# Sums of exponentials read over 112 columns, one divisor operation, partition copies on GpSimd, and a new instruction order, in a fused attention and gated MLP kernel

## The chip, the cores and the metric

The kernel runs on one core of a Trainium2 chip. Its time is the device time of one launch in microseconds. Three runs gave 727.54, 728.48 and 729.30 us, median 728.48.

Engines are named as in the profile: PE is TensorE's matrix multiply, PEld its weight load, DVE is VectorE, ACT is ScalarE, POOL is GpSimd, SP is the engine that issues nearly all DMAs.

## The reference

Eight batches, twelve heads, 448 positions, head size 64. Attention with a soft cap, then a gated MLP with a spatial product, all in float32:

```python
scores = matmul(q, k.T) / sqrt(64)
scores = cap * tanh(scores / cap)
attn = exp(scores - max(scores))
attn = attn / (sum(attn) + 1e-9)
x = matmul(attn, v)                      # heads side by side: 448 x 768
h = maximum(x @ w_in, 0)                 # 448 x 1024
u, v = h[:, :512], h[:, 512:]
v_n = (v - mean(v)) / sqrt(var(v) + 1e-6)
v_s = w_spatial @ v_n + b_spatial[:, None]
out = (u * v_s) @ w_out                  # 448 x 768
```

## The kernel before, in words

**Two programs.** One branch serves a small cap, where exp needs no maximum subtracted beforehand; the other serves any cap. The branch is taken once, on the chip. All that is told here is of the first (`bounded`).

**Attention, `pair_bnd` (L556).** Heads are worked two at a time: six pairs per batch, 48 in all. Scores are computed transposed, keys on partitions and 448 queries of two heads on columns, in 64-row by 64-column tiles of the PE array (L593, 56 matmuls of 224 columns a pair, each in two passes in the trace). ACT takes tanh into `tp` (key blocks 0 to 3) and `tq` (blocks 4 to 6) (L600) and exp in place (L605). PE multiplies with the values (L615) into `ps_x`, again in 64 by 64 tiles; ACT copies that to `xf` (L620).

**The divisor.** The maximum of the exponentials is always made on DVE (L647 four tensor operations, L658 a 32 by 32 transpose, L660 a reduce into `st`). It is needed for the 1e-9 term. The sum of the exponentials is made on PE for the first ten pairs (`PE_SUMS = 10`, all of batch 0 and four pairs of batch 1), by products with a matrix of ones (L640): for each of seven key blocks, four products of 128 columns that lie side by side in four 32-column strips of the array, one for each head and each of two overlapping groups of 32-query blocks. ACT copies the result to `sx` (L644). One of the ten (pair 5, `FAST`) goes on through PE; the other nine go through DRAM: `sx` to `sd` to `dq` by DMA. For those nine, DVE then moves the upper halves of `st` to other partitions (L705, two copies of 32 by 14), takes the maximum (L714), forms the divisor in two operations (L711) and its reciprocal (L716), and two more DMA steps bring the reciprocal to all partitions as `rr`. In the other 38 pairs DVE makes the sums too.

**The MLP, `moe` (L784).** `xf` times `rr` (L773) is split in two float32r parts `xg` (ACT or DVE, L352, L348, and for batch 0 a copy of 64 columns on DVE, L354). PE computes u and v (L806 to L808, L828 to L833), the spatial product (L901 to L906) and the output (L926 to L928) with three float32r products for each, on the whole 128 by 128 array. The weights are split from float64 in the first 120 us, on POOL (L419), DVE (L423 to L426, L348) and ACT (L352).

**What sets the order.** Every step is a `Plan` task with an engine, a duration, a key and the buffers it needs. `Plan.order` (L75) plays the tasks through a list scheduler once, on the host: an idle engine takes the ready task of the smallest key, PE adds `STICK` to the key of a task whose array mode differs from the last one's, and POOL and some DVE tasks exclude each other. The result is one fixed order for each engine; on the chip each engine runs its list in order and waits on semaphores. The keys are the tables `BND_KEY`, `KEY0`, `KEY1`, `KEY7` (added for batches 0, 1 and 7) and `BND_W_KEYS`.

Of the kernel before, what the change touches and what calls it, by code (L numbers as in the profile page):

```python
# [18 lines left out]
FH = DF // 2  # L19
# [26 lines left out]
class Plan:  # L46
# [7 lines left out]
    TURN, STICK = {"N": 111.0, "K": 95.0, "R": 190.0, "C": 100.0, "Q": 100.0}, 11.80957  # L54
# [174 lines left out]
BND_KEY = dict(tr=-300.859619, ld=66.923828, vld=74.281982, sc=-6.748779, th=-13.830078, ex=-614.690186, pv=1.041748, sm=26.029053, mx=26.478027, dn=31.365723, ev=-123.362305, x=5.41333, moe=9.348389, span=8.481445, step=0.303955, mv=-3.17041)  # L229
KEY0 = dict(tr=59.859619, ld=-206.415527, vld=-222.091553, sc=-619.906494, th=-404.370117, ex=637.646729, pv=-43.61792, sm=472.690186, mx=-388.116455, dn=-437.234619, ev=-178.652832, x=-259.482666, moe=-7.794922, mv=-2.662842)  # L230
KEY1 = dict(tr=409.030762, ld=-17.121582, vld=-89.626709, sc=-8.86792, th=-12.678955, ex=103.096191, pv=-3.411865, sm=-34.066406, mx=-33.196045, dn=-141.463135, ev=-64.928467, x=-7.304688, moe=-0.158936, mv=-9.574707)
KEY7 = dict(tr=-794.004639, ld=1184.412354, vld=279.873779, sc=0.273438, th=878.253174, ex=671.313232, pv=-1.608398, sm=35.75708, mx=35.69043, dn=-2.840088, ev=359.308594, x=2.395508, moe=-0.6604, mv=169.783203)
BND_V_FIRST = 1
WARM, WARM_N = 7, 480
BND_W_KEYS = -12.596436, 0.300049, -1.349609, -18.415039, 10.094727
# [9 lines left out]
VH3 = True  # L245
# [3 lines left out]
def attn_moe(ctx, tc, bounded, shared, qk, v, qk2, v2, cap, w_in, w_sp, w_out, out):  # L249
# [12 lines left out]
    const = pool("const", 1)  # L262
    if bounded and VH3:
        TAGS = {**TAGS, "vh": (512, F32R, 3)}
# [298 lines left out]
    def pair_bnd(b, hp, xf):  # L563
# [67 lines left out]
        if by_pe:  # L631
            acc, sx = Buf("acc"), Buf("sx")
            bank = lambda: acc.t[:, 0]
            sides = [(k, e) for k in range(2) for e in range(2)]

            def ones():
                for c in range(NC):
                    for s, (k, e) in enumerate(sides):
                        o = bank()[s * 32:(s + 1) * 32, :128]
                        nc.tensor.matmul(o if fast else o.rearrange("p (i b) -> p b i", b=4), lhsT=one, rhs=part(c, e)[:, k * 96:k * 96 + 128],  # L640
                                         start=(c == 0), stop=(c == NC - 1))

            z1 = add("T", 1540, kk("pv", 1) + 0.01, ones, exps, [*tps, acc], [acc], name="ones", mode="Q")
            z1 = add("A", act(128), kk("ev"), lambda: nc.scalar.copy(out=sx.t, in_=bank()[:, :128]), [z1], [acc, sx], [sx], name="sev")  # L644
# [49 lines left out]
        if by_pe and SHIFT:  # L694
# [4 lines left out]
                       [sx, sd], [sd], lat=XL)  # L699
            sums = [add("S", HW, kk("dn"), lambda h=h: nc.sync.dma_start(  # L700
                out=dq.t[half_h(h), :16].rearrange("p (s b) -> p s b", b=4),
                in_=sd.t.rearrange("(s h i b) -> h i s b", h=2, i=32, b=4)[h]), [sums], [sd, dq], [dq] if h == 0 else [], lat=XL) for h in range(2)]

            def shift(h):
                nc.vector.tensor_copy(low(0)[half_h(h)], st.t[h * D + 32:h * D + D, :QB])  # L705

            def den(k):
                b = slice(0, 4) if k == 0 else slice(4, 7)
                i, o = (low(j).rearrange("p (e b) -> p e b", e=2)[:, :, b] for j in (1, 2))
                a = dq.t[:96, :16].rearrange("p (s b) -> p s b", b=4)[:, 2 * k:2 * k + 2, k:]  # L710
                nc.vector.scalar_tensor_tensor(o, i, EPS_ATTN, a, op0=ALU.mult, op1=ALU.add)  # L711

            d = [add("V", 90, kk("dn"), lambda h=h: shift(h), [*done, sums[0]], [st, dq], name="shift") for h in range(2)]
            d = add("V", 90, kk("dn"), lambda: nc.vector.tensor_tensor(low(1), st.t[:96, :QB], low(0), op=ALU.max), d, [st, dq], name="mred2")  # L714
            d = [add("V", 105, kk("dn"), lambda k=k: den(k), [d, *sums], [dq], name="den") for k in range(2)]
# [43 lines left out]
    def pair(b, hp):  # L759
# [16 lines left out]
        t = add(E_X[3], ct(E_X[3], D), k, lambda: copy(E_X[3], g.t[:, S:XH], xf.t[:, S - D:]), [m, c], [xf, g], name="xt")  # L776
# [10 lines left out]
    def moe(b, xs):  # L787
# [27 lines left out]
        def v_part():  # L815


            for t in range(4):
                k = next(ks)
                acc, vr, ls, vh, vl = Buf(next(tags)), Buf("stg"), Buf("lst"), Buf("vh3" if bounded and VH3 and t == 3 else "vh"), Buf("vl")  # L820
                ts, last = slice(t * 128, (t + 1) * 128), t == 3

# [192 lines left out]
```

## Time and profile before

| What | Time (us) |
|---|---|
| median of three runs | 728.48 |
| the profiled execution | 728.05 |
| its span, first to last instruction | 726.3 |
| PE busy | 712.7 |
| DVE busy | 603.0 |
| ACT busy | 475.2 |
| POOL busy | 40.0 |

The profiled execution lies 0.43 us under the median. PE is busy 98% of the span, at the full granted clock all through (1.00 in every stretch until the last matmul). Busy time counts a matmul from start to end, and matmuls overlap, so a busy PE may still lose time where it changes between tile shapes; that is read from start times.

### The profile page before, as it was taken

The numbers are of one execution on the slowest core, as the hardware profiler recorded it, in microseconds if no ns is written. First come the engines' busy times: TensorE is split into PE (matmuls) and PEld (weight loads), VectorE is DVE, ScalarE is ACT, GpSimd is POOL, SyncE is SP. The second block draws the span as 40 slices with busy tenths as digits, with TensorE's granted clock in tenths as the row PEclk, the third lists the DMA queues.
The fourth block names the chain that finished last, engine by engine and source line by source line (L and its number), as shares of the span: only waits on it lengthen the run. The fifth ranks groups of instructions, "written<-read, shape, count | busy, mean of one in ns | idle before, by whom it ended". The sixth has DMA issues, their size and how long they took to land.

```text
span 726.3 us, 19114 instructions
## 1 busy us (share of the span) xinstructions
PE 712.7 (98%) x8001; PEld 596.5 (82%) x8001; DVE 603.0 (83%) x1187; ACT 475.2 (65%) x658; POOL 40.0 (6%) x57
## 2 busy tenths in 40 slices
PE   8998999999999999999999999999999999999997
PEld 5776788788898888887788887988889887888896
DVE  4999999999998999797997899978988869874530
ACT  7998757876829848479466676576582874572321
POOL 2301110000100010000100000000000001000100
PEclk9999999999999999999999999999999999999999
DMA  7577724443404414135133443144241441212002
GB/s 262 177 209 232 220 59 122 136 144 93 128 19 155 153 34 130 53 130 157 37 97 92 128 120 76 58 129 141 69 130 28 143 123 65 66 41 98 8 0 81
DMA packets 53286, 78.87 MB, mean 109 GB/s; under 512 B 24956, under 2 KB 37830, under 8 KB 53190
## 3 DMA queue, kind: packets, MB, share of 16 engines
q1 hardware_dynamic: 53044, 77.55, 35.7%
q8 instruction: 65, 1.06, 0.6%
q14 instruction: 31, 0.25, 0.1%
q10 hardware_dynamic: 146, 0.00, 0.0%
HBM read 65.76 MB, written 11.76 MB: 107 GB/s over the span
## 4 chain that ended last, share of the span: by engine, by line
PE 81%; DVE 10%; ACT 3%; DMA 3%; issue 1%; POOL 0%; SPq 0%; ACTq 0%; DVEq 0%; POOLq 0%
PE ps_s L593 14%; PE ps_x L615 14%; PE ps_acc L926 5%; PE ps_acc L928 5%; PE ps_acc L927 5%; PE ps_acc L806 4%; PE ps_acc L808 4%; PE ps_acc L807 4%; PE ps_acc L831 4%; PE ps_acc L833 4%; PE ps_acc L832 4%; DVE red L647 4%; PE ps_acc L904 2%; PE ps_acc L906 2%; PE ps_acc L905 2%; PE ps_acc L828 1%
## 5 line engine op out<-in xcount | busy, mean ns | idle before, releaser
L647 DVE TENSOR_TENSOR red<-red,tq 128x896 f32<-128x896 f32 (+1 forms) x172 | 141.9, 847 | 24.1 <-ACT tq L605 24.1
L593 PE MATMUL ps_s<-raw 64*64 64x224 f32 x2688 | 147.8, 353 | 3.3 <-ACT tp L600 1.4
L593 PEld LDWEIGHTS ps_s<-raw 64*64 64x64 f32 x2688 | 98.1, 133 | 39.4 <-ACT tp L600 5.8
L600 ACT ACTIVATE tp<-ps_s,capt 128x896 f32<-128x896 f32 x96 | 92.0, 1012 | 3.5 <-PE ps_s L593 2.3
L647 DVE TENSOR_TENSOR red<-tp 128x896 f32<-128x896 f32 x86 | 90.6, 1077 | 4.4 <-ACT tp L605 4.4
L605 ACT ACTIVATE tp<-tp,capt 128x1792 f32<-128x1792 f32 x48 | 86.6, 1804 | 0.5
L615 PE MATMUL ps_x<-tp,v 64*64 64x224 f32 x1536 | 81.6, 350 | 1.5 <-ACT tp L605 1.2
L600 ACT ACTIVATE tq<-ps_s,capt 128x896 f32<-128x896 f32 x96 | 73.7, 822 | 10.6 <-PE ps_s L593 9.3
L615 PEld LDWEIGHTS ps_x<-tp,v 64*64 64x64 f32 x1536 | 57.8, 133 | 17.2 <-ACT tp L605 1.6
L605 ACT ACTIVATE tq<-tq,capt 128x1344 f32<-128x1344 f32 x48 | 68.4, 1425 | 0.9
L926 PE MATMUL ps_acc<-xg,wo_h 128*128 128x448 f32 x176 | 64.6, 367 | 0.0
L615 PE MATMUL ps_x<-tq,v 64*64 64x224 f32 x1152 | 63.2, 349 | 1.1 <-ACT tq L605 1.1
L806 PE MATMUL ps_acc<-xg,wiu_h 128*128 128x448 f32 x174 | 64.0, 368 | 0.0
L928 PE MATMUL ps_acc<-xg,wo_l 128*128 128x448 f32 x176 | 63.8, 363 | 0.0
L927 PE MATMUL ps_acc<-xg,wo_h 128*128 128x448 f32 x176 | 63.5, 361 | 0.0
L808 PE MATMUL ps_acc<-xg,wiu_l 128*128 128x448 f32 x174 | 63.1, 363 | 0.0
L807 PE MATMUL ps_acc<-xg,wiu_h 128*128 128x448 f32 x174 | 62.7, 360 | 0.0
L773 DVE TENSOR_TENSOR xf<-xf,rr 128x448 f32<-128x448 f32 x47 | 29.0, 618 | 30.5 <-DMA rr<-rd 21.6
L855 POOL TENSOR_TENSOR lst<-lst,capt 128x1 f32<-128x1 f32 x32 | 21.6, 678 | 585.2 <-DVE lst L853 481.7
L615 PEld LDWEIGHTS ps_x<-tq,v 64*64 64x64 f32 x1152 | 43.9, 133 | 11.9 <-ACT tq L605 1.5
L658 DVE STREAM_TRANSPOSE red<-red 128x448 f32<-128x448 f32 x85 | 52.7, 632 | 0.6
L647 DVE TENSOR_TENSOR red<-red 128x448 f32<-128x448 f32 x86 | 52.2, 620 | 0.2
(144 smaller groups left out, 1298.1 us busy)
## 6 DMA issues: line engine op xcount, KB each, us to landing
v<-in_v SPq DMA_DIRECT2D x48, 448.0 KB, 4.7
raw<-in_qk SPq DMA_DIRECT2D x47, 448.0 KB, 4.4
out<-o SPq DMA_DIRECT2D x48, 224.0 KB, 2.3
rr<-rd SPq DMA_DIRECT2D x94, 112.0 KB, 3.1
w<-in_w_in SPq DMA_DIRECT2D x12, 512.0 KB, 5.0
xg<-in_w_out SPq DMA_DIRECT2D x12, 256.0 KB, 2.9
wy<-in_w_sp SPq DMA_DIRECT2D x3, 224.0 KB, 3.3
md<-st SPq DMA_DIRECT2D x38, 14.0 KB, 1.7
```

The costliest lines, as they stand in the source:

```text
L593: nc.tensor.matmul(ps.t[half_rows(h), e, c % 2 * QH:(c % 2 + 1) * QH], lhsT=raw.t[half_rows(e), S + c * D:S + (c + 1) * D], rhs=raw.t[half ...
L600: lambda o=g % 2 * PW, w=w, ps=ps, tp=tp: nc.scalar.activation(out=tp.t[:, o:o + 2 * w].rearrange("p (e q) -> p e q", e=2), in_=ps.t[:, :, ...
L605: lambda tp=tp, w=w: nc.scalar.activation(out=tp.t[:, :w], in_=tp.t[:, :w], func=AF.Exp, scale=ca), [ex], [tp],
L615: nc.tensor.matmul(inat(x.t[half_rows(e), h, :QH]), lhsT=vt.t[half_rows(h), (2 * c + e) * D:(2 * c + e + 1) * D], rhs=part(c, e)[half_rows ...
L647: tt = lambda o_, i0, i1, op=op: nc.vector.tensor_tensor(o_, i0, i1, op=op)
L658: d = add("V", dve(S) + 26, kk(key), lambda r=r, one_=one_: nc.vector.transpose(out=blk(r.t[:, :S]), in_=blk(one_())), [d], [r], name="vtr")
L806: nc.tensor.matmul(ps, lhsT=wiu_h[:, c, fs], rhs=x[:, XH:], start=(c == 0), stop=False)
L807: nc.tensor.matmul(ps, lhsT=wiu_h[:, c, fs], rhs=x[:, :S], start=False, stop=False)
L808: nc.tensor.matmul(ps, lhsT=wiu_l[:, c, fs], rhs=x[:, XH:], start=False, stop=(c == NP - 1))
L926: nc.tensor.matmul(ps, lhsT=wo_h[:, c, ns], rhs=g[:, XH:], start=(c == 0), stop=False)
L927: nc.tensor.matmul(ps, lhsT=wo_h[:, c, ns], rhs=g[:, :S], start=False, stop=False)
L928: nc.tensor.matmul(ps, lhsT=wo_l[:, c, ns], rhs=g[:, XH:], start=False, stop=(c == 3))
```

## The change

It has four parts.

**Ones.** For the nine pairs that go through DRAM, each product with ones reads 16 of the 32 queries of each of all seven 32-query blocks (112 columns in seven runs of 16) instead of four whole blocks (128 columns in one run). `sx` has 112 columns, the two heads go to `sd` in two DMAs, and each of the two DMAs to `dq` waits for its own.

**Divisor.** With that layout the divisor is one operation over 14 columns where there were two, over 8 and 6.

**Partition copies.** The two copies of `st` to other partitions (`E_SHIFT`), and in batch 0 the copy of 64 columns of `xf` into `xg` (`E_XT`), are issued on POOL instead of DVE.

**Order.** All key tables have new values, so the order changes on every engine for batches 0, 1 and 7 above all. The other new names (`LN_A`, `ST_A`, `RL_A`) are zero and change nothing.

```diff
-    TURN, STICK = {"N": 111.0, "K": 95.0, "R": 190.0, "C": 100.0, "Q": 100.0}, 11.80957
+    TURN, STICK = {"N": 111.0, "K": 95.0, "R": 190.0, "C": 100.0, "Q": 100.0}, 12.158936
-BND_KEY = dict(tr=-300.859619, ld=66.923828, vld=74.281982, ...
+BND_KEY = dict(tr=-120.344971, ld=111.291992, vld=156.294922, ...
...
-VH3 = True
+E_SHIFT, E_DEN, E_XT, E_EPS = "P", "V", "P", "V"
+SMALL = 150
+LN_A, ST_A, RL_A, VH3, W112 = 0, 0, 0, True, True
...
-            sides = [(k, e) for k in range(2) for e in range(2)]
+            sides = [(k, e) for k in range(2) for e in range(2)] if not W112 or fast else [(k, e) for e in range(2) for k in range(2)]
...
+                        if W112 and not fast:
+                            nc.tensor.matmul(o[:, :QC].rearrange("p (i b) -> p b i", b=QB // 2), lhsT=one,
+                                             rhs=part(c, e).rearrange("p (b i) -> p b i", i=32)[:, :, k * 16:k * 16 + 16],
+                                             start=(c == 0), stop=(c == NC - 1))
+                            continue
                         nc.tensor.matmul(o if fast else o.rearrange("p (i b) -> p b i", b=4), lhsT=one, rhs=part(c, e)[:, k * 96:k * 96 + 128],
                                          start=(c == 0), stop=(c == NC - 1))
...
-            z1 = add("T", 1540, kk("pv", 1) + 0.01, ones, exps, [*tps, acc], [acc], name="ones", mode="Q")
+            z1 = add("T", 1360 if W112 and not fast else 1540, kk("pv", 1) + 0.01, ones, exps, [*tps, acc], [acc], name="ones", mode="Q")
...
             def shift(h):
-                nc.vector.tensor_copy(low(0)[half_h(h)], st.t[h * D + 32:h * D + D, :QB])
+                copy(E_SHIFT, low(0)[half_h(h)], st.t[h * D + 32:h * D + D, :QB])
 
             def den(k):
+                if W112:
+                    nc.vector.scalar_tensor_tensor(low(2), low(1), EPS_ATTN, dq.t[:96, :QB], op0=ALU.mult, op1=ALU.add)
+                    return
...
-        t = add(E_X[3], ct(E_X[3], D), k, lambda: copy(E_X[3], g.t[:, S:XH], xf.t[:, S - D:]), [m, c], [xf, g], name="xt")
+        e_xt = E_XT if bounded and E_X[3] == "V" else E_X[3]
+        t = add(e_xt, SMALL + 30 if e_xt == "P" else ct(e_xt, D), k, lambda: copy(e_xt, g.t[:, S:XH], xf.t[:, S - D:]), [m, c], [xf, g], name="xt")
```

Where the instructions now stand is shown at three places. The first is ACT's list at the end of the first stage, where attention of batch 0 runs out and the first MLP product follows on PE (`tp` and `tq` are exponentials, `ps_s` the scores, `wiv_h` and `wiu_h` weight parts, `xg` a finished pair). Before:

```order
L605 ACTIVATE tq<-tq,capt 128x1344
L620 COPY xf<-ps_x 128x448
L352 CAST wiv_h<-wy 128x512
L600 ACTIVATE tp<-ps_s,capt 128x896
L352 CAST xg<-xf 128x448 x2
L644 COPY sx<-ps_acc 128x128
L600 ACTIVATE tp<-ps_s,capt 128x896
L352 CAST wiv_h<-wy 128x512
L605 ACTIVATE tp<-tp,capt 128x1792
```

Now:

```order
L609 ACTIVATE tq<-tq,capt 128x1344
L624 COPY xf<-ps_x 128x448
L356 CAST wiv_h<-wy 128x512
L604 ACTIVATE tp<-ps_s,capt 128x896 x2
L356 CAST wiv_h<-wy 128x512
L609 ACTIVATE tp<-tp,capt 128x1792
L653 COPY sx<-ps_acc 128x112
L356 CAST xg<-xf 128x448 x2
L356 CAST wiv_h<-wy 128x512
```

The last two casts of `xg` in batch 0 moved behind the second tanh, a weight cast, the exp of `tp` and a copy of `sx`.

The second place is DVE from the first reduce into `st` to the maximum over the halves. Before, the two copies `dq<-st` stand on DVE:

```order
L660 TENSOR_REDUCE st<-red_172 128x14
L647 TENSOR_TENSOR red_173<-tp 128x896
L426 SCALAR_TENSOR_TENSOR wy<-w_215,wy 128x512
L423 TENSOR_SCALAR wy<-wy 128x512 x2
L424 SCALAR_TENSOR_TENSOR wy<-w_217,wy 128x512
L647 TENSOR_TENSOR red_173<-red_173,tq 128x896
L426 SCALAR_TENSOR_TENSOR wy<-w_217,wy 128x512
L647 TENSOR_TENSOR red_173<-red_173 128x448
L348 TENSOR_TENSOR wiu_l<-wy,wiu_h 128x512
L647 TENSOR_TENSOR red_173<-red_173,tq 128x448
L705 COPY dq_175<-st 32x14 x2
L658 STREAM_TRANSPOSE red_173<-red_173 128x448
```

Now DVE has none there, and POOL has them between two weight steps; this is POOL's list:

```order
L423 TENSOR_SCALAR wy<-w_229 128x512
L360 TENSOR_SCALAR dq_175<-st 32x14 x2
L423 TENSOR_SCALAR wy<-w_387 128x512
L423 TENSOR_SCALAR wy<-w_431 128x512
L360 TENSOR_SCALAR dq_176<-st 32x14 x2
L423 TENSOR_SCALAR wy<-w_558 128x512
L360 TENSOR_SCALAR xg<-xf 128x64
```

The copies moved to POOL's queue, where each pair stands behind a weight step; DVE's maximum, which stands ten operations after the reduce, waits for POOL.

The third place is PE in the output products of batch 0's neighbour, batch 1. Before, they run on without a break:

```order
L926 MATMUL ps_acc<-xg,wo_h 128x448
L927 MATMUL ps_acc<-xg,wo_h 128x448
L928 MATMUL ps_acc<-xg,wo_l 128x448
L926 MATMUL ps_acc<-xg,wo_h 128x448
L927 MATMUL ps_acc<-xg,wo_h 128x448
L928 MATMUL ps_acc<-xg,wo_l 128x448
```

Now scores stand between the second group of three and the next:

```order
L967 MATMUL ps_acc<-xg,wo_h 128x448
L968 MATMUL ps_acc<-xg,wo_h 128x448
L969 MATMUL ps_acc<-xg,wo_l 128x448
L597 MATMUL ps_s<-raw_62 64x224 x16
L967 MATMUL ps_acc<-xg,wo_h 128x448
L968 MATMUL ps_acc<-xg,wo_h 128x448
L969 MATMUL ps_acc<-xg,wo_l 128x448
```

One group of scores moved into the run, and with it PE goes from whole-array products to 64 by 64 tiles and back once more. Over the whole list of PE such passages from 64 by 64 tiles to whole-array products number 25 before and 30 now, and the passages back 24 and 28.

## Rows read from the trace of the kernel before

**Rows 1.** Windows: busy us (instructions) PE, PEld, DVE, ACT, POOL; granted clock; DMA.
```profile
0.00:74.30 74.30, 67.49 (x1433) 49.49 (x1433) 62.54 (x133) 67.07 (x82) 15.08 (x23) 1.00 0.71 218
74.30:160.00 85.70, 84.83 (x918) 70.04 (x918) 83.32 (x190) 62.42 (x100) 6.06 (x6) 1.00 0.48 138
160.00:599.50 439.50, 439.48 (x4808) 371.22 (x4801) 384.56 (x724) 295.21 (x398) 13.33 (x20) 1.00 0.34 101
```
**Rows 2.** Waits of PE from 74.3 us on: total us, times, longest.
```profile
PE ps_acc L833 <- DVE xg L348: 0.7, 1, 0.7
PE ps_x L615 <- ACT xf L620: 0.3, 1, 0.3
```
**Rows 3.** Timeline of PE, 14 to 17 us: start, us, line, tile, shape, count.
```profile
14.74 1.08 PE L640 MATMUL ps_acc<-tp,one 128*32 128x128 f32 x32
15.64 0.84 PE L640 MATMUL ps_acc<-tq,one 128*32 128x128 f32 x24
```
**Rows 4.** Durations (min/median/max ns), L640 and L677, by source line.
```profile
L640 PE MATMUL ps_acc<-tp,one x320: 272/273/297, 14.7 to 111.0; 128*32 128x128 f32 x160
...
L677 PEld LDWEIGHTS ps_acc<-ident,st x16: 132/137/137, 61.5 to 62.2; 128*64 128x64 f32 x16
L677 PE MATMUL ps_acc<-ident,st x16: 246/259/322, 61.5 to 62.3; 128*64 128x128 f32 x8, 128*64 128x96 f32 x8
```
**Rows 5.** Timeline of PE: what follows those L677 products.
```profile
62.45 0.42 PE L593 MATMUL ps_s<-raw 64*64 64x224 f32 x4
```
**Rows 6.** Timeline of PE, 156 to 168 us: to 64 by 64 tiles and back.
```profile
156.51 0.36 PE L928 MATMUL ps_acc<-xg,wo_l 128*128 128x448 f32 x1
156.80 1.37 PE L593 MATMUL ps_s<-raw 64*64 64x224 f32 x24
157.98 1.69 PE L615 MATMUL ps_x<-tp,v 64*64 64x224 f32 x32
159.50 1.69 PE L593 MATMUL ps_s<-raw 64*64 64x224 f32 x32
...
165.93 1.69 PE L593 MATMUL ps_s<-raw 64*64 64x224 f32 x32
167.55 0.50 PE L831 MATMUL ps_acc<-wiv_h,xg 128*128 128x512 f32 x1
167.89 0.40 PE L832 MATMUL ps_acc<-wiv_l,xg 128*128 128x512 f32 x1
168.12 0.40 PE L833 MATMUL ps_acc<-wiv_h,xg 128*128 128x512 f32 x1
```
**Rows 7.** Timelines of ACT and of PE before the first MLP product.
```profile
70.31 1.03 ACT L352 CAST xg<-xf 128x448 fp32r<-128x448 f32 x2
...
71.41 1.01 ACT L600 ACTIVATE tp<-ps_s,capt 128x896 f32<-128x896 f32 x1
72.31 0.61 ACT L352 CAST wiv_h<-wy 128x512 fp32r<-128x512 f32 x1
...
74.35 0.47 PE L806 MATMUL ps_acc<-xg,wiu_h 128*128 128x448 f32 x1
```
**Rows 8.** Waits of ACT, 12 to 73 us.
```profile
ACT xg L352 <- DVE xf L773: 2.0, 3, 1.0
...
ACT xf L620 <- DVE xg L354: 0.4, 1, 0.4
```
**Rows 9.** Groups of DVE that the change moves or merges: busy, mean ns.
```profile
L705 DVE COPY dq<-st 32x14 f32<-32x14 f32 x18 | 4.9, 272 | 0.6
L711 DVE SCALAR_TENSOR_TENSOR dq<-dq 96x8 f32<-96x8 f32 x9 | 1.4, 157 | 0.1
```
**Rows 10.** Timelines of POOL and DVE, 27 to 42 us.
```profile
27.67 5.06 POOL L419 TENSOR_SCALAR wy<-w 128x512 f32<-128x512 f32 x1 [3.48 <-DVE wiu_l L348]
40.17 1.03 POOL L419 TENSOR_SCALAR wy<-w 128x512 f32<-128x512 f32 x1 [7.45 <-DVE wiu_l L348]
40.54 1.22 DVE L424 SCALAR_TENSOR_TENSOR wy<-w,wy 128x512 uint32<-128x512 uint32 x1
```

More of the change, by code (lines that the diff above doesn't have):

```diff
@@ L262, in attn_moe @@
     const = pool("const", 1)
+    if bounded and ST_A:
+        sq = const.tile([128, 512], F32, name="sq")
     if bounded and VH3:
@@ L639, in ones @@
                         o = bank()[s * 32:(s + 1) * 32, :128]
+                        if W112 and not fast:
[3 more added lines that the diff above has]
+                            continue
                         nc.tensor.matmul(o if fast else o.rearrange("p (i b) -> p b i", b=4), lhsT=one, rhs=part(c, e)[:, k * 96:k * 96 + 128],
                                          start=(c == 0), stop=(c == NC - 1))
-            z1 = add("T", 1540, kk("pv", 1) + 0.01, ones, exps, [*tps, acc], [acc], name="ones", mode="Q")
-            z1 = add("A", act(128), kk("ev"), lambda: nc.scalar.copy(out=sx.t, in_=bank()[:, :128]), [z1], [acc, sx], [sx], name="sev")
+            z1 = add("T", 1360 if W112 and not fast else 1540, kk("pv", 1) + 0.01, ones, exps, [*tps, acc], [acc], name="ones", mode="Q")
+            z1 = add("A", act(128), kk("ev"), lambda: nc.scalar.copy(out=sx.t[:, :QC if W112 and not fast else 128], in_=bank()[:, :QC if W112 and not fast else 128]), [z1], [acc, sx], [sx], name="sev")
         for a, op, key in ((0, ALU.max, "mx"), (1, ALU.add, "sm"))[:1 if by_pe else 2]:
@@ L821, in v_part @@
                 ts, last = slice(t * 128, (t + 1) * 128), t == 3
+                ln_a, st_a, rl_a = (bounded and b < n for n in (LN_A, ST_A, RL_A))
+                acc_ = lambda ls=ls: {"accum_out": ls.t[:, 6:7]} if st_a else {}
                 def vm(c, acc=acc, ts=ts, last=last):
@@ L852, in v_part @@
[L852 to L854 removed]
+                    if rl_a or st_a:
+                        r = add("A", act_s(512, st_a), kv(k), lambda v2=v2, acc_=acc_: nc.scalar.activation(out=v2(), in_=v2(), func=AF.Relu, **acc_()),
+                                [r], [vr, *([ls] if st_a else [])], [ls] if st_a else [], name="vrelu")
+                    else:
+                        r = add("V", dve2(512), kv(k), lambda v2=v2: nc.vector.tensor_scalar(v2(), v2(), 0.0, None, op0=ALU.max), [r], [vr],
+                                name="vrelu")
+                else:
+                    r = add("A", act(512, st_a), kv(k), lambda acc=acc, v2=v2, acc_=acc_: nc.scalar.activation(
+                        out=v2(), in_=acc.t[:, 0], func=AF.Relu, **acc_()), [l], [acc, vr], [vr, ls] if st_a else [vr], name="vrelu")
@@ L855, in v_part, with norm @@
                 s2 = add("P", 464, kv(k), lambda ls=ls: nc.gpsimd.tensor_tensor(ls.t[:, 9:10], ls.t[:, 8:9], half, op=ALU.pow), [s1],
                          [ls])
-                def norm(v2=v2, ls=ls):
+                if ln_a:
+                    s2 = add("P", 250, kv(k), lambda ls=ls: nc.gpsimd.tensor_scalar(ls.t[:, 10:11], ls.t[:, 6:7], ls.t[:, 9:10], -1.0, op0=ALU.mult, op1=ALU.mult), [s2], [ls])
+                def norm(v2=v2, ls=ls, ln_a=ln_a):
+                    if ln_a:
+                        nc.scalar.activation(out=v2(), in_=v2(), func=AF.Identity, scale=ls.t[:, 9:10], bias=ls.t[:, 10:11])
+                        return
```

51 lines of the change are left out of this document (32 added, 19 removed).

## The prediction

> **What bounds the kernel now.** I read the windows by stage first. Up to 74.3 us PE is busy for 67.49 us, ACT for 67.07, DVE for 62.54; from 74.3 to 160 us PE is busy for 84.83 of 85.70 us, and from 160 to 599.5 us for all but 0.02 [rows 1]. So there are two kinds of stage. In the first, PE has only the attention of batch 0 and waits for ACT's tanh and exp; ACT and DVE run nearly without a break. After 74.3 us PE has MLP products to fill with and sets the time itself: there only fewer or shorter matmuls, fewer passages between tile shapes, or the removal of one of its few waits can help. The waits of PE from there on are four: one of 0.7 us on DVE's `xg`, and three of 0.3 us of which one stands in the group [rows 2], 1.6 us in all.
>
> So I forecast two things: when PE starts its first MLP product (L806, at 74.35 us [rows 7]), and what the rest costs.
>
> **The ones.** A pair has 28 products, 56 records (each product runs in two passes), four side by side in the strips. The 32 records from 14.74 us on take until 15.64 us [rows 3], that is 0.90 / 8 = 112 ns for each four. In L677, which mixes 128 and 96 columns, the shortest record takes 246 ns where 128 columns take 272 [rows 4]: 26 ns for 32 columns, so 13 ns for 16. Fourteen fours a pair: 14 x 13 = 0.18 us a pair, 1.7 us for nine. Could the weight load set the pace instead, so that nothing is gained? The sixteen L677 records, two at a time, need eight rounds of loads of 137 ns; one after the other that is 1.10 us, but from 61.54 us, the start that the group gives as 61.5, to the next product at 62.45 us there are only 0.91 [rows 4, 5]. So loads overlap, and I take 13 ns; the bounds are 0 and 13. No row reads columns in seven runs. Bounds: nothing, or at worst half speed, which would add some 80 ns to each four and 10 us to nine pairs. In the trace the products that write in steps (L640, nine of ten pairs) and those that write in one run (the tenth) lie within 272 to 297 ns [rows 4], so I take nothing.
>
> The Trainium skill, "TensorE: Matmul & The Clock Gate", section "Wait — 56ns, not 53.3ns?", says that matmuls never start less than about 25 ns apart. By it a four would need 100 ns and save 9 instead of 13. The trace does not decide: 112 ns for four are 28 on average, and no row has a shorter product in strips. By the rule the two later pairs would give 0.25 us instead of 0.4.
>
> Where do these 1.7 us count? Seven of the nine pairs have their ones before the first MLP product, in the stage where PE waits for ACT. There 7 x 0.18 = 1.3 us turn into waiting. Two pairs come later: **-0.4 us**.
>
> **The start of the first MLP product.** It follows the second matmul group with `tq` of the eighth pair, which stands behind a score group that needs the bank freed by ACT's tanh at 71.41 us [rows 7]. From that tanh's end at 72.42 to 74.35 us are 1.9 us, the same in both orders, since the same matmuls lie between. What changes is what stands before that tanh on ACT. By the order shown in the change, two casts of `xg` and one copy of `sx` moved behind it: 71.41 - 70.31 = 1.1 us [rows 7]; one more weight cast stands ahead, 0.6 us [rows 7]. So it is 0.5 us earlier, before ACT's waits are counted.
>
> Will the casts then be late? They now follow a weight cast (0.6), an exp of `tp` and a copy. A tanh of 896 columns takes 1.01 us [rows 7], so that exp, over 1792, at most 2.0, and the copy with the first cast about 0.7. So the first of the two casts ends some 3.3 us after the tanh; PE needs that pair after 1.9 + 12 products of 0.2 = 4.3 us, and DVE's subtraction between takes some 0.6. A margin of 0.3 to 0.4 us: just in time, and no term.
>
> ACT's waits: between 12 and 73 us it waited 2.0 us for DVE's product `xf` and 0.4 for DVE's copy into `xg` [rows 8]. DVE loses the 18 copies (4.9 us, 272 ns each) and nine of 18 divisor operations (nine x 157 ns = 1.4 us) [rows 9], some 6 us in all over 110 us, two thirds of them in this stage. DVE's products should come ahead of ACT's need, and the copy into `xg` is now POOL's. But POOL and DVE disturb each other: beside a POOL step of 1.03 us the DVE step at 40.54 took 1.22 us [rows 10], about twice its usual length. If each of the 20 or so POOL operations of this stage costs DVE 0.05 to 0.3 us, 1 to 6 us come back. Bounds for ACT's waits: all 2.4 us gone, or 1.5 us more than before. I take 1.4 us gone, nearer the first, since the waits had been on single steps. First MLP product: 0.5 + 1.4 = **-1.9 us**, at about 72.4 us.
>
> **Passages.** At 156.80 us PE goes to 64 by 64 tiles 0.29 us after the last wide start, usually 0.20, and its first 24 records take 1.18 us where 32 take 1.52, so 0.04 over: 0.13. Back: 165.93 to 167.55 us are 1.62, 0.10 over, and the first wide product takes 0.34 where the next takes 0.23: 0.21 [rows 6]. Five more passages to wide products and four more back: 5 x 0.21 + 4 x 0.13 = **+1.6 us**. All of them lie after 74 us, where PE has nothing to hide them.
>
> **Waits after 74 us.** 1.6 us can go [rows 2]. The long one, in batch 6, stands at a product whose place has not changed, but DVE now makes the two products of that pair without a reduce between, so it comes some 0.5 us earlier. Of the 0.3 us ones all three lie where the order is new. I take **-1.2 us**; bounds -1.6 and, with new waits, +0.5.
>
> **Other edits.** Nine more DMAs go through SP; the steps to `dq` read 28-byte runs where they read 16. They lie behind matmul work and cost nothing unless `rr` is late, and then DVE waits as in the slower rival. The end of the program keeps its list: after the last product with `tq` PE runs wide products to the end, and needs the last pair 15 products of 0.23 us later, 3.4 us, where before it was 12.
>
> **Sum.** -1.9 - 0.4 + 1.6 - 1.2 = -1.9 us. On the profiled execution (728.05) that is 726.15; that execution lies 0.43 under the median of the three, so **726.6 us**. Its own range, with ACT's waits between 0.5 and 2.4 gone, is 725.0 to 728.0.
>
> **Rivals.**
>
> *Wash.* ACT's waits stay (0.2 gone) and half of PE's later waits: -0.7 - 0.4 + 1.6 - 0.6 = -0.1, **728.4 us**. For it: the passages cost for certain, the gains hang on waits.
>
> *POOL is held out.* One mechanism: POOL's copies stand behind weight steps in one queue, and one such step took 5.06 us [rows 10] while DVE ran two-input operations back to back; another of the same shape took 1.03. DVE's maximum then waits for the copy, and behind it all reductions and weight steps, for which ACT waits. It decides when the wait passes what a pair saves: 2 x 0.272 + 0.157 + a copy into `xg`, about 0.8 us. At 1.5 us a pair, six pairs of the first stage lose 4 us net; then ACT waits 1.5 us more instead of 1.4 less: +1.0 - 0.4 + 1.6 + 0 = +2.2, **730.7 us**. Against it: the maximum stands ten operations after the reduce, which is several us. The Trainium skill, "SBUF — State Buffer", section "Who interferes with whom", says that the port pair which GpSimd and VectorE share is an exclusive lock, held for a whole instruction, and that VectorE operations with two SBUF inputs contend for it with GpSimd reads. The 5.06 us row agrees with that rule. It gives this rival its chance.
>
> *More than that.* DVE's relief lets ACT wait for nothing (2.4 gone), and all of PE's waits go: -2.9 - 0.4 + 1.6 - 1.6 = -3.3, **725.2 us**, and down to 724 if part of the passages falls into waits.
>
> **How the numbers follow.** Forecast 0.47, wash 0.20, POOL 0.16 (with the small chance that reading in runs is slow), more 0.17. What this kernel's measurement can tell from no change is about 0.2%, 1.46 us: faster is under 727.0, slower above 729.9. The forecast is near that line, so 0.30 of it is faster and 0.17 the same. Faster 0.30 + 0.17 = 0.47; same 0.17 + 0.20 = 0.37; slower 0.16. Range: from below the largest gain, 724.0, to the slower rival, 730.6.
>
> **What would show it.** L640's successor at about 260 ns a record and about 0.18 us shorter a pair. The first product of `u` at 72.4 us; at 74 or later the first step is wrong. PE's later waits under 0.5 us. POOL's copies of `dq` at a few tenths each; several at over 2 us, with DVE idle before L735, would make the slower rival true. PE start times around the new passages with 0.3 us a round trip.

## The result and the profile after

The changed kernel takes **734.09 us** (five runs, 732.42 to 736.60) against 728.48 (five runs, 727.46 to 729.30): ratio **1.0075** [1.0052, 1.0098]. It is slower, 7.5 us above the forecast of 726.6 and above the range. The profiled execution took 732.8 us with a span of 730.9, 4.6 us more than the span before; it lies 1.3 us under the median of the five.

The windows of the kernel after, by the same stages and with the same columns as [rows 1]:

```profile
0.00:74.30 74.30, 65.79 (x1396) 46.84 (x1400) 58.38 (x109) 65.30 (x80) 24.38 (x37) 1.00 0.70 215
74.30:160.00 85.70, 84.52 (x932) 70.48 (x927) 81.36 (x176) 59.54 (x97) 10.42 (x16) 1.00 0.44 131
160.00:599.50 439.50, 438.75 (x4798) 368.01 (x4794) 385.76 (x726) 297.49 (x400) 11.33 (x20) 1.00 0.35 101
```

DVE did less in the first stage, 58.38 us where it had 62.54. Part of that is work which in this window had not been reached; over the whole span DVE is 3.9 us lighter (599.1 where it was 603.0). PE and ACT also did less in the first stage (65.79 and 65.30 where they had 67.49 and 67.07): they waited longer. And in the long middle stage, where PE had lost 0.02 us, it now loses 0.75.

The timeline of PE around the first MLP product, which answers to the last row of [rows 7]:

```profile
75.66 0.72 PE L619 MATMUL ps_x<-tq,v 64*64 64x224 f32 x6
76.31 0.48 PE L830 MATMUL ps_acc<-xg,wiu_h 128*128 128x448 f32 x1
```

76.31 us, where 72.4 was forecast and 74.35 stood before. So 1.96 us of the 4.6 are lost before this product, 2.7 behind it.

The waits of ACT between 12 and 73 us (total us, times, longest), where [rows 8] stood:

```profile
ACT xf L624 <- POOL xg L360: 3.0, 2, 1.6
ACT wiu_h L356 <- DVE wy L430: 1.0, 1, 1.0
ACT xg L356 <- DVE xf L796: 0.4, 1, 0.4
```

The waits for DVE's product `xf` nearly went, from 2.0 to 0.4 us, as forecast. In their place stand 3.0 us for POOL's copies into `xg` and 1.0 us for a weight step. Timelines of POOL, ACT and PE around the first of the two long ones, and of DVE in the same microseconds and beside the copy at 49.89 (start, us, line, tile, shape; in brackets the idle time before and what ended it):

```profile
38.49 5.25 POOL L360 TENSOR_SCALAR xg<-xf 128x64 fp32r<-128x64 f32 x1 [3.75 <-DVE xf L796]
43.71 0.64 POOL L423 TENSOR_SCALAR wy<-w 128x512 f32<-128x512 f32 x1
...
49.89 0.24 POOL L360 TENSOR_SCALAR xg<-xf 128x64 fp32r<-128x64 f32 x1 [4.96 <-DVE xf L796]
...
57.37 2.71 POOL L360 TENSOR_SCALAR xg<-xf 128x64 fp32r<-128x64 f32 x1 [2.44 <-DVE dq L739]
```

```profile
38.47 0.62 DVE L428 SCALAR_TENSOR_TENSOR wy<-w,wy 128x512 uint32<-128x512 uint32 x1
39.02 0.41 DVE L427 TENSOR_SCALAR wy<-wy 128x512 uint32<-128x512 uint32 x1
39.34 1.08 DVE L656 TENSOR_TENSOR red<-red,tq 128x896 f32<-128x896 f32 x1
...
42.55 1.08 DVE L656 TENSOR_TENSOR red<-tp 128x896 f32<-128x896 f32 x1
43.56 0.63 DVE L667 STREAM_TRANSPOSE red<-red 128x448 f32<-128x448 f32 x1
...
49.66 0.61 DVE L669 TENSOR_REDUCE st<-red 128x14 f32<-128x448 f32 x1
```

```profile
43.77 0.53 ACT L624 COPY xf<-ps_x 128x448 f32<-128x448 f32 x1 [1.58 <-POOL xg L360]
...
44.36 1.74 PE L619 MATMUL ps_x<-tp,v 64*64 64x224 f32 x32 [1.82 <-ACT xf L624]
```

All waits of PE for that copy out of PSUM, up to the first product of `u`:

```profile
PE ps_x L619 <- ACT xf L624: 2.8, 2, 1.8
```

Read them from top to bottom. The copy of 64 columns takes 0.24 us at 49.89, while DVE runs a reduce with one input, and 5.25 us at 38.49. In those 5.25 us DVE runs eight operations without a break; the copy ends 0.18 us after the transpose has begun. In dq_dve and tail_old, two of the experiments below, the same copy takes 5.26 and 5.25 us and also ends 0.18 and 0.19 us after the start of the transpose. ACT's next copy out of PSUM goes into the buffer of `xf` that POOL is still reading, so ACT stands still for 1.58 us, and PE, which needs that PSUM bank, for 1.82. The Trainium skill, "SBUF — State Buffer", section "Who interferes with whom", says that GpSimd and VectorE share one port pair as an exclusive lock, and that VectorE's operations with two SBUF inputs, and copies and `tensor_scalar` in its two-port modes, contend for it. The trace agrees as far as it shows: seven of the eight have two inputs in SBUF, the eighth is a `tensor_scalar` of 0.41 us (in which mode it ran no row says), and the copy gets through at the transpose, which has one input.

The ones, by source line, and in the timeline of PE, where [rows 3, 4] stood:

```profile
L645 PE MATMUL ps_acc<-tp,one x288: 259/259/284, 15.1 to 114.1; 128*32 128x112 f32 x144
```
```profile
15.10 0.97 PE L645 MATMUL ps_acc<-tp,one 128*32 128x112 f32 x32
15.89 0.76 PE L645 MATMUL ps_acc<-tq,one 128*32 128x112 f32 x24
```

259 ns a record where it was 272 or 273, and 0.79 us for the 32 where it was 0.90: 99 ns for each four, 14 less. Reading in seven runs costs PE nothing. The rule that the prediction cites from the Trainium skill, "TensorE: Matmul & The Clock Gate", section "Wait — 56ns, not 53.3ns?", starts not less than about 25 ns apart, does not describe products side by side in strips here: by the single records those of a four start 7 ns apart, before and after, and most fours follow the last after 96 ns, where they did after 109. The measurement decides.

PE's waits from 74.3 us on, where [rows 2] stood:

```profile
PE ps_s L597 <- ACT tq L604: 1.1, 2, 0.6
PE ps_s L597 <- ACT tp L604: 0.6, 1, 0.6
PE ps_acc L830 <- ACT sx L653: 0.6, 1, 0.6
```

The one on DVE's `xg` is gone, as forecast. But scores now wait for the tanh of the scores before them, until 115.5, 169.5 and 617.6 us, 1.7 us in all, and a product of `u` waits 0.6 us for a copy of sums. That is 2.3 us in this list where 1.6 stood.

### The profile page after: what moved, and what is told of

It reads as the page before. It is cut to its first block, busy times and chain, and to the rows that moved or that the text cites. A ratio compares the mean times of both kernels' runs of the same rounds, so it can differ in the third digit from the quotient of the medians.

```text
span 730.9 us, 19147 instructions
## 1 busy us (share of the span) xinstructions
PE 714.7 (98%) x8001; PEld 594.1 (81%) x8001; DVE 599.1 (82%) x1154; ACT 475.6 (65%) x658; POOL 51.2 (7%) x81
## 4 chain that ended last, share of the span: by engine, by line
PE 70%; DVE 14%; DMA 8%; ACT 3%; issue 2%; POOL 1%; SPq 1%; DVEq 0%; ACTq 0%; POOLq 0%
PE ps_s L597 11%; PE ps_x L619 11%; DVE red L656 5%; PE ps_acc L967 4%; PE ps_acc L830 4%; PE ps_acc L969 4%; PE ps_acc L968 4%; PE ps_acc L832 4%; PE ps_acc L831 4%; PE ps_acc L857 3%; PE ps_acc L858 2%; PE ps_acc L859 2%; PE ps_acc L945 2%; PE ps_acc L947 2%; PE ps_acc L946 2%; DMA rr<-rd 2%
## 5 line engine op out<-in xcount | busy, mean ns | idle before, releaser
L656 DVE TENSOR_TENSOR red<-red,tq 128x448 f32<-128x448 f32 (+1 forms) x172 | 143.5, 854 | 26.4 <-ACT tq L609 26.2
L604 ACT ACTIVATE tq<-ps_s,capt 128x896 f32<-128x896 f32 x96 | 74.3, 822 | 9.2 <-PE ps_s L597 8.7
L891 POOL TENSOR_TENSOR lst<-lst,capt 128x1 f32<-128x1 f32 x32 | 19.4, 607 | 569.9 <-DVE lst L889 539.9
L857 PE MATMUL ps_acc<-wiv_h,xg 128*128 128x512 f32 x132 | 52.5, 397 | 0.0
```

What stands on the lines that cost most here:

```text
L604: lambda o=g % 2 * PW, w=w, ps=ps, tp=tp: nc.scalar.activation(out=tp.t[:, o:o + 2 * w].rearrange("p (e q) -> p e q", e=2), in_=ps.t[:, :, ...
L656: tt = lambda o_, i0, i1, op=op: nc.vector.tensor_tensor(o_, i0, i1, op=op)
L857: nc.tensor.matmul(ps, lhsT=x[:, XH:][:, ts], rhs=wiv_h[:, c], start=(c == 0), stop=False)
```

## The experiments

All are compared with the kernel before. Most edits change only which engine an instruction is issued on, or what it reads, and keep the order of the program, so that nothing else moves. Runs of one kernel differ by 2 to 9 us, so the ratios decide and the profile shows the mechanism. The last two columns come from the one profiled execution of each kernel, which lies up to 3 us from its median; the last is the span behind the start of that product.

| kernel | ratio, 95% interval | first product of `u`, us | from there, us |
|---|---|---|---|
| before | 1 | 74.35 | 651.9 |
| after | 1.0075 [1.0052, 1.0098] | 76.31 | 654.6 |
| xg_dve | 1.0038 [1.0020, 1.0056] | 74.61 | 655.1 |
| dq_dve | 1.0069 [1.0044, 1.0094] | 77.47 | 657.1 |
| both_dve | 1.0069 [1.0042, 1.0097] | 78.79 | 656.9 |
| order_alone | 1.0093 [1.0063, 1.0123] | 77.12 | 655.5 |
| b_w112 | 1.0021 [1.0007, 1.0035] | 74.34 | 652.0 |
| b_dq_pool | 1.0004 [0.9991, 1.0016] | 76.81 | 652.4 |
| b_xg_pool | 1.0008 [0.9992, 1.0024] | 74.39 | 652.0 |
| b_all | 1.0001 [0.9985, 1.0017] | 72.19 | 650.6 |
| head_old | 1.0136 [1.0109, 1.0163] | 79.80 | 655.6 |
| head_old2 | 1.0072 [1.0049, 1.0095] | 73.36 | 657.4 |
| tail_old | 1.0028 [1.0007, 1.0048] | 78.06 | 650.7 |
| fix_head | 1.0030 [1.0016, 1.0045] | 74.27 | 656.0 |
| fix_head_tail_old | 1.0011 [0.9997, 1.0025] | 74.42 | 652.9 |
| b_cast | 1.0047 [1.0032, 1.0063] | 75.59 | 652.9 |
| b_all_cast | 1.0055 [1.0038, 1.0071] | 76.81 | 655.5 |
| b_all_sev | 1.0040 [1.0021, 1.0059] | 74.98 | 653.6 |
| b_noshift | 0.9969 [0.9948, 0.9990] | 73.47 | 650.5 |
| b_sub_pool | 1.0090 [1.0065, 1.0116] | 77.22 | 657.2 |

### Parts taken back in the new order

**xg_dve**

```diff
-lambda: copy(e_xt, g.t[:, S:XH], xf.t[:, S - D:])
+lambda: copy(E_X[3], g.t[:, S:XH], xf.t[:, S - D:])
```
Expected:

> The changed kernel, its order kept; only the six copies into xg (64 columns, batch 0) go from GpSimd back to VectorE, at the same place in the program. Theory A (held copies: a copy on GpSimd waits beside VectorE's two-input operations, one took 5.25 us, and ScalarE waited 3.0 us for two of them): those 3.0 us of ScalarE's wait go, the first product of u starts at about 73.3 us instead of 76.3, the time is 730 to 731.5 us. Theory B (the new order itself costs: passages and new waits for tanh and exp): the first product stays at 75.5 us or later, the time at 733 us or more.

The wait for POOL is gone and half of the loss with it: 0.37 points, some 2.7 us (0.1 to 0.7 points by the two intervals). The held copies are real and are worth that much where the rest of the change stands. The other half is not theirs: 74.61 us for the first product is neither Theory A's 73.3 nor Theory B's 75.5.

**dq_dve**

```diff
-copy(E_SHIFT, low(0)[half_h(h)], st.t[h * D + 32:h * D + D, :QB])
+copy("V", low(0)[half_h(h)], st.t[h * D + 32:h * D + D, :QB])
```
Expected:

> The changed kernel, its order kept; only the 18 copies into dq (14 columns, nine pairs) go from GpSimd back to VectorE. Theory A: VectorE's waits for them (1.1 us) go and 18 x 0.27 = 4.9 us of work come back; GpSimd's queue is free for the xg copies, but these are still held: 733 to 735 us. Theory B: the same, 733 to 735 us. If the dq copies in GpSimd's queue were what delays the xg copies, it would be 731 us.

As both theories had it: little changes. POOL's first copy into `xg` takes 5.26 us here too, with no `dq` copy in the queue, so it is not the queue that holds it. **both_dve**, with both edits, was expected to be:

> The changed kernel, its order kept, with both kinds of copies on VectorE. Theory A: ScalarE's 3.0 us go, VectorE has 6 us more: 730 to 732 us, first product of u at 73.3 to 74.3 us. Theory B: 733 to 735 us.

It is no better than dq_dve, which Theory A had not expected: with the `dq` copies on DVE, taking the `xg` copies from POOL wins nothing. A reason that fits is that DVE, with all its old work back, is itself late for ACT, which in this trace waits 1.9 us for weight steps and 1.8 for `xf` and `xg`. It is not shown: the trace is of the slowest of six executions, 2.4 us over their median, and in it PE also stands still for 1.2 us that the profile puts down to nobody. **order_alone** puts the old instructions into the new order:

```diff
-                        if W112 and not fast:
-                            nc.tensor.matmul(o[:, :QC].rearrange("p (i b) -> p b i", b=QB // 2), lhsT=one,
...
-                if W112:
-                    nc.vector.scalar_tensor_tensor(low(2), low(1), EPS_ATTN, dq.t[:96, :QB], op0=ALU.mult, op1=ALU.add)
-                    return
+                if k == 2:
+                    return [den(j) for j in range(2)]
```

> The instructions of the kernel before (ones over 128 columns, two divisor operations, all copies on VectorE) in the order of the changed kernel. Theory A: 728.5 plus the passages between tile shapes (1.6 us) and PE's waits after 74 us (1.0 more than before): about 731 us, first product of u at 74 to 75 us. Theory B: 734 us or more, first product of u at 76 us or later.

Theory B holds: the order by itself costs 0.93%. The other three parts may win 0.2 points of it back; the two intervals overlap.

### Parts in the old order

**b_w112**, **b_dq_pool**, **b_xg_pool** and **b_all** are the kernel before with the ones and the divisor, with either kind of copy on POOL, and with all three:

```diff
-nc.vector.tensor_copy(low(0)[half_h(h)], st.t[h * D + 32:h * D + D, :QB])
+copy("P", low(0)[half_h(h)], st.t[h * D + 32:h * D + D, :QB])
...
-lambda: copy(E_X[3], g.t[:, S:XH], xf.t[:, S - D:])
+lambda: copy("P" if bounded and E_X[3] == "V" else E_X[3], g.t[:, S:XH], xf.t[:, S - D:])
```

> The kernel before in its own order, with the ones over 112 columns and one divisor operation, all copies on VectorE as before. Theory B (the new order costs, the parts themselves gain): ones 14 ns shorter a record, 0.36 us less after the first product of u, nine divisor operations less on VectorE; 0.4 to 1.5 us under the kernel before. Theory C (reading in seven runs, or the two smaller DMAs in place of one, disturbs the first stage): equal to the kernel before or slower.

> The kernel before in its own order, with only the 18 copies into dq on GpSimd. Theory B: VectorE has 4.9 us less work and waits a few tenths for some copies; within 0.7 us of the kernel before, either side. Theory A (copies on GpSimd are held by VectorE's two-input operations): VectorE waits before its maximum, 1 to 3 us slower.

> The kernel before in its own order, with only the copies into xg of batch 0 on GpSimd. Theory A: one or two of them take over 2 us beside VectorE's two-input operations, ScalarE waits for them 1 us or more, 1 to 3 us slower. Theory B: copies of 0.3 to 0.7 us, within 0.7 us of the kernel before.

> All three parts of the change in the order of the kernel before: ones over 112 columns with one divisor operation, dq and xg copies on GpSimd. Theory B (only the order cost time): 0.5 to 2 us under the kernel before. Theory A (the copies on GpSimd cost the most): 1 to 4 us over the kernel before.

None gains; Theory B's 0.5 to 2 us for all three did not come. b_w112 is even 0.2% over, as its Theory C had it; its profile, at the time and the first product of the kernel before, does not show where, so the cause stays open. In b_xg_pool one copy into `xg` took 3.78 us, and nobody waited for it, but only just: it ended at 39.68 us, and ACT's next copy into `xf` began at 39.71. A held copy costs only where someone stands behind it. In b_dq_pool DVE no longer makes the copies, 14 of 272 ns in the first stage or 3.8 us, and waits instead:

```profile
DVE xf L773 <- DMA rr<-rd: 3.7, 3, 1.9
DVE dq L714 <- POOL dq L356: 2.9, 4, 1.1
DVE red L647 <- ACT tq L605: 1.7, 1, 1.7
```

These are its waits from 12 to 73 us: 2.9 for the copies that it no longer makes, and 3.7 for `rr`, which comes back from DRAM behind the divisor that follows on them (1.0 in the kernel before). This execution took 731.02 us, 3 more than the median of b_dq_pool, and in it PE's granted clock was at the lower level from 38.6 to 42.0 us, after PE had stood still for 2.9 us; in that of b_all, at 724.83 the fastest of its twelve, DVE still waits 2.5 us for the copies in the same stretch.

### Both orders in one program

To split the cost of the order I issued the changed kernel's instructions by a list in which one stretch has the old order:

```diff
-        for t in plan.order():
+        for t in ([plan.tasks[i] for i in ORDER] if bounded else plan.order()):
```

> The instructions of the changed kernel (112 columns, one divisor operation, copies on GpSimd), issued in the order of the kernel before up to the first product of u and in the new order from there. Theory D (both stretches of the new order cost time: the first by ScalarE's waits for a weight step and for held copies, the later one by three more passages each way between tile shapes, 0.28 us a round trip, and some 1 us of new waits): 1.5 to 3 us over the kernel before (ratio 1.002 to 1.004), first product of u at 72 to 75 us. Theory E (only the first stretch costs): within 1 us of the kernel before.

This one failed for a reason of its own: in my list the second of a pair's two sums DMAs stood where the first step to `dq` belongs. There is one buffer for `sx`, so ACT could not write the next sums until that DMA had gone:

```profile
ACT sx L653 <- DMA sd<-sx: 5.1, 1, 5.1
```

It says nothing on the theories, but it shows what a late DMA in SP's queue costs a buffer with one copy. With the DMA in its place (**head_old2**):

> Again the changed kernel's instructions in the order of the kernel before up to the first product of u and in the new order from there, now with the second of a pair's two sums DMAs right behind the first (in the earlier mixture it was issued in the place of a step to dq, and ScalarE waited 5.1 us for it). Theory D (both stretches of the new order cost): ratio 1.002 to 1.005, first product of u at 72 to 75 us, from there to the end 3 to 4 us more than in the kernel before. Theory E (only the first stretch costs): ratio 0.999 to 1.001.

**tail_old**, the reverse:

> The instructions of the changed kernel in the new order up to the first product of u, and in the order of the kernel before from there. Theory D: 2 to 3.5 us over the kernel before (ratio 1.003 to 1.005), first product of u at 76 us or later, from there to the end as in the kernel before or 0.4 us less. Theory E: 5 us over it (ratio 1.007).

Theory D holds in kind: both stretches cost. Its sizes don't. Behind the old head the new order costs 0.72% alone, 5.5 us in the last column where 3 to 4 were expected; tail_old, with the new head alone, has 0.28%. Going back to the old order in the later stretch takes 0.47 points off the changed kernel, but only 0.19 off fix_head (below), which its intervals do not tell from nothing. So that the later stretch is the larger part is clear with two heads of three, and the shares do not add up. The last column of the table points the same way: behind the first product of `u` the seven programs with the old order there and nothing but parts of the change in them (from before to fix_head_tail_old) need 650.6 to 652.9 us, the eight with the new order 654.6 to 657.4, on average 4.2 us more, without overlap. (The order isn't all that can lengthen it: b_all_cast and b_sub_pool have the old order there and need 655.5 and 657.2 us.)

**fix_head** and **fix_head_tail_old** put three things right in the new head:

```diff
-L574 DMA raw_174<-in_qk 128x896
 L577 DMA v<-in_v 128x896 x2
+L574 DMA raw_174<-in_qk 128x896
...
-L356 CAST wiu_h<-wy 128x512 x2
+L356 CAST wiu_h<-wy 128x512
 L604 ACTIVATE tq<-ps_s,capt 128x896
 L604 ACTIVATE tq<-ps_s,capt 128x448
+L356 CAST wiu_h<-wy 128x512
```

These are SP's and ACT's lists; the third edit is that of xg_dve.

> The changed kernel with three things put right in its first stretch: the copies into xg on VectorE, the first loads of v ahead of the second pair's raw, and ScalarE's second cast into wiu_h behind the next tanh. Theory D: against the kernel with only the copies on VectorE (ratio 1.0038) the 1 us wait of ScalarE for the weight step goes and the first tanh starts 0.3 us earlier: ratio 1.002 to 1.003, first product of u at 73 to 74 us. Theory E: ratio 1.000 to 1.001.

> The same three things put right, and from the first product of u on the order of the kernel before. Theory D: 0.3 to 2 us under the kernel before (ratio 0.997 to 0.9995). Theory E: the same as with the new order behind it, ratio 1.000 to 1.001. If both are wrong and the new first stretch is long for another reason: ratio 1.002 or more.

Theory D's 1.002 to 1.003 for the first came; the second ends at 1.0011, not under 1. xg_dve alone has 1.0038, and the intervals overlap, so it is not shown that the other two corrections gain anything. The cast I moved no longer waits, but a later cast into `wiu_h` does, 1.2 us until 32.25, for another of DVE's weight steps: the wait moved on.

### What sets the first stage

In the old order the parts had given nothing. Is it that DVE's time is worth nothing, or that POOL gave it back? And is ACT the limit? **b_cast** and **b_all_cast** move the eight casts of weights from ACT to DVE, **b_all_sev** the copy of the sums:

```diff
-(ew[1], ct(ew[1], n), lambda: copy(ew[1], hi, yf())),
+(ew[1], ct(ew[1], n), lambda: copy("V" if bounded and not late else ew[1], hi, yf())),
...
-nc.scalar.copy(out=sx.t[:, :128 if fast else QC], in_=bank()[:, :128 if fast else QC])
+nc.vector.tensor_copy(sx.t[:, :128 if fast else QC], bank()[:, :128 if fast else QC])
```

> The kernel before with one edit: the eight casts of the first MLP weights (128 x 512, 0.63 us each) go from ScalarE to VectorE, order kept. If ScalarE's work alone set the first product of u: 3 us earlier, ratio 0.996. If VectorE, with its 62 us of work in the first 74, is as much a limit: ratio 1.000 to 1.005.

> All three parts of the change in the order of the kernel before, and the eight casts of the first MLP weights on VectorE instead of ScalarE. Theory F (VectorE's relief is worth something only where ScalarE, which has 67 us of work in the first 74, is relieved as well): first product of u at 70 to 72 us, ratio 0.995 to 0.998. Against it: VectorE's chain of reductions and divisor steps becomes late, ratio 1.000 or more.

> All three parts of the change in the order of the kernel before, and the copy of the sums out of PSUM on VectorE instead of ScalarE (0.25 us each, seven in the first stretch). Theory F: ScalarE has 1.7 us less to do, ratio 0.997 to 0.999. Against it: VectorE, in its own order, waits for the ones and is late with the reductions: ratio 1.001 or more.

All three are slower; Theory F's forecasts fall. ACT's longest waits from 12 to 73 us, in b_cast and, the two lines behind, in b_all_cast:

```profile
ACT xg L352 <- DVE xf L773: 5.1, 4, 1.7
```
```profile
ACT xg L352 <- DVE xf L779: 4.2, 4, 1.4
ACT xf L620 <- POOL xg L356: 3.2, 1, 3.2
```

5.1 and 4.2 us where 2.0 stood [rows 8]. In b_all_cast one copy into `xg` is held for 6.30 us as well, and here, in the old order, ACT stands 3.2 us behind it, so that this run is not a test of Theory F alone. ACT looked like the limit by its busy time, but what it waits for is the end of DVE's chain, and every step added there comes back to it. **b_noshift** takes the 18 copies away and puts them nowhere; **b_sub_pool** gives POOL steps that nobody needs for long:

```diff
-nc.vector.tensor_copy(low(0)[half_h(h)], st.t[h * D + 32:h * D + D, :QB])
+pass
```
```diff
-(ew[2], st2(ew[2], n), lambda: sub(ew[2], lo, yf(), f(hi))),
+(ew[2], st2(ew[2], n), lambda: sub("P" if bounded and not late else ew[2], lo, yf(), f(hi))),
```

> The kernel before with its 18 copies into dq left out altogether (the maximum then reads what the buffer held, so this part of the divisor isn't computed), order kept. Theory G (VectorE's time sets the first stretch, and the copies on GpSimd gave their relief back as VectorE's waits for them, 4.0 us in the kernel with all three parts): 14 copies of 0.27 us fewer in that stretch bring its end 1.5 to 3.5 us forward, ratio 0.995 to 0.998. Theory H (the relief itself is worth nothing, the stretch hangs on ScalarE and the round trips through DRAM): ratio 0.999 to 1.001.

> The kernel before with the subtractions for the low parts of the first MLP weights (128 x 512, eight on VectorE before the first product of u, 0.61 us each) on GpSimd, order kept; nobody needs them before that product. Theory G: VectorE has some 4 us less to do and waits for none of them, ratio 0.995 to 0.998. Theory H: 0.999 to 1.001. If GpSimd's steps with two inputs are held by VectorE's, or slow them, as the copies were: later weight steps on GpSimd are late, ratio 1.002 or more.

b_noshift is the only faster one, 0.31%, 2.2 us: DVE's time is worth something (Theory G), and the same copies on POOL bring 1.0004. So POOL gave the relief back. The size in the first stretch is under Theory G's 1.5 to 3.5 us: in its trace the first product comes 0.9 us earlier, and the rest lies behind it. In b_sub_pool, POOL's subtractions slow DVE. DVE's group of the reductions with `tq`, 12 to 73 us, busy and mean ns, there and in the kernel before:

```profile
L647 DVE TENSOR_TENSOR red<-red,tq 128x896 f32<-128x896 f32 (+1 forms) x14 | 15.2, 1086 | 1.8 <-ACT tq L605 1.7
```
```profile
L647 DVE TENSOR_TENSOR red<-red,tq 128x896 f32<-128x896 f32 (+1 forms) x14 | 11.9, 849 | 1.7 <-ACT tq L605 1.7
```

DVE's 3.3 us more here take up most of the subtractions it was freed of. Of the seven over 448 columns, three that run beside a subtraction take 1.58 to 1.59 us; the others take 0.59 to 0.63. Behind the first product of `u`, this kernel's 657.2 us have another cause too, a wait of PE and a lower clock after it (last section).

## Why the prediction was wrong

**The ones: right.** 14 ns a four; behind the first product of `u` their starts add up to 2.58 us where they did to 2.93, the forecast 0.4. The 9 ns and 0.25 us by the rule on starts go by fours 109 ns apart, not by the 112 of the text; both are under what came.

**The first MLP product: this step failed.** It was to come 1.9 us earlier and came 1.96 later. Its main term was that 1.4 us of ACT's waits go, with a bound on the other side of "1.5 us more than before". ACT's waits were 2.9 us (the prediction's 2.4 and one of 0.5 for the ones) and are 4.4: 1.5 more, at that bound. I had seen that an operation on POOL can be held, [rows 10], and asked only who waits for the copies of `dq`. Those took 0.33 us in the median, and DVE waited 1.1 us for two. I set "the copy into `xg` is now POOL's" down as a gain without asking who waits for the buffer that it reads: ACT, three operations later. PE waits for ACT there in turn, 2.8 us for two copies out of PSUM; all its pauses from 4 us to the product add up to 7.4 us where they did to 5.7. The other 0.5, from ACT's order, did not come either: the second pair's `raw` now loads ahead of `v`, the first tanh starts 0.36 us later, and a cast placed earlier waits 1.0 us for its weight step. That I counted a weight cast as 0.6 us and not as a wait on DVE is the same omission. And the path was wrong: the product was to follow 1.9 us after the tanh, "the same in both orders". Now 24 records of scores lie behind that tanh where 8 did, PE runs without a pause from 60.7 us to the product, and from the tanh's end at 73.17 us to the product are 3.1 us. An earlier tanh there would have brought nothing; what counts is what PE lost before.

**Passages: right.** Behind the first product of `u`, PE's records show 28 passages to whole-array products where there were 23, and 27 to 64 by 64 tiles where there were 23: five and four more, as counted in the prediction. (One passage goes to the strips of the ones as well. The three each way in the expectation of head_old are a miscount.) Against the usual distances of starts a passage costs 0.15 us to the tiles and 0.22 back, forecast 0.13 and 0.21, and together they cost 1.65 us more than before, forecast 1.6.

**Waits after 74 us: the second step that failed, wrong in sign.** -1.2 us was forecast, with +0.5 as the worst. The 0.7 us on `xg` did go, but this stretch takes 2.65 us more; less 1.65 for the passages, and with the 0.35 that the ones save, 1.35 us of new waits are left. 0.7 of it is in the list of waits, the rest in pauses too short for it. The list holds scores that wait for tanh. I had taken new places in PE's order as a chance to lose waits and not as a place for new ones; in the mixtures this stretch costs 4.2 us on average, of which the passages are the same 1.65. Which moved task makes tanh late there wasn't tried and stays open.

Together: 1.96 - 0.35 + 1.65 + 1.35 = 4.6 us, the difference of the two spans, where -1.9 was forecast. (The forecast's own range, 725.0 to 728.0 us, is a little wider than ACT's waits between 0.5 and 2.4 us give, 725.6 to 727.5; the miss does not hang on that.)

**The rivals.** *POOL is held out* named the mechanism and priced it at 730.7 us with 0.16: right in kind, but on the copies of `xg` and with ACT waiting, and without the later stretch, from which most of the rest comes. Its sign, several copies of `dq` at over 2 us with DVE idle before L735, did not come: the longest of them took 0.92 us, and DVE waited 1.1 us there. The copies of 5.25 and 2.71 us, at 38.49 and 57.37, are those into `xg`. That its 730.7 us lies nearer to the result than the forecast is in part luck.

**Runs of the changed kernel** lie 4.2 us apart. Those of the kernel before lie 1.8 us apart in the same series, but nearly all within some 6 us in the later ones, so a wider spread is not shown. The slowest of the five, 736.60 us, had a mean granted clock of 0.996 and the fastest, 732.42, of 0.999. One way to such a difference shows elsewhere. In the profile of tail_old the same copy took 5.25 us, PE then waited 3.08 us, and the timeline of PE and the windows around it (columns as above) show what follows:

```profile
44.55 3.10 PE L619 MATMUL ps_x<-tp,v 64*64 64x224 f32 x32 [3.08 <-ACT xf L624]
47.41 1.71 PE L619 MATMUL ps_x<-tq,v 64*64 64x224 f32 x24
```
```profile
40.00:44.00 4.00, 1.47 (x56) 1.23 (x56) 4.00 (x7) 1.54 (x3) 4.00 (x2) 1.00 0.68 178
44.00:48.00 4.00, 3.45 (x40) 2.56 (x44) 2.54 (x5) 4.00 (x6) 0.96 (x3) 0.60 0.74 249
48.00:52.00 4.00, 4.00 (x110) 3.07 (x108) 3.47 (x9) 3.47 (x5) 0.24 (x1) 0.98 0.38 115
```

After the idle stretch the granted clock is 0.60 in the mean, nearer the lower of its two levels (1.2 and 2.4 GHz). Here the wait was paid for twice: the 32 products behind it took 2.86 us to the next start, where they took 1.56 in the trace of the changed kernel, after its wait of 1.82 us. That the longer runs of the changed kernel went this way is not shown, since this trace is of another kernel.

## What to carry to other kernels

Before moving a small copy to GpSimd, list who waits for what it writes *and* who will overwrite what it reads, and look at what VectorE runs beside it: here the price was not the copy's 0.24 us but the length of VectorE's unbroken run of two-input operations, and it counted only where someone stood behind. Judge a new order separately before and behind the point where the bound changes; a list of both orders, cut there, tells the two apart at the price of a few runs. And ask first what a saving on one engine of a chain is worth, by leaving the work out: what that gives in the same order (here 0.3%) is a guide to the most that moving it can give.

## What the runs showed of the hardware that was not expected

POOL and DVE hold each other up in both directions. Beside DVE's long runs POOL's copy of 64 columns grew from 0.24 to 5.25 us, in b_all_cast to 6.30; beside POOL's subtractions DVE's reductions grew from 849 to 1086 ns in the mean. And PE's granted clock fell to the lower of its two levels after single waits of some 3 us: in tail_old after 3.08 us, and in b_sub_pool, where PE waited 2.94 us for tanh until 87.23 us and the granted clock was 0.56 from 86 to 90 us and 0.59 in the next 4:

```profile
87.23 2.52 PE L593 MATMUL ps_s<-raw 64*64 64x224 f32 x24 [2.94 <-ACT tp L600]
```
```profile
82.00:86.00 4.00, 2.29 (x51) 1.53 (x40) 3.97 (x6) 1.47 (x3) 2.26 (x2) 1.00 0.12 24
86.00:90.00 4.00, 2.77 (x32) 1.89 (x36) 3.55 (x7) 3.80 (x4) 0.00 (x0) 0.56 0.41 129
90.00:94.00 4.00, 4.00 (x76) 2.87 (x72) 1.02 (x3) 1.27 (x3) 1.27 (x1) 0.59 0.72 199
```
